# Row norms by powers on GpSimd in place of logarithms and exponentials on ScalarE

## The chip, the cores and the metric

The kernel runs on one core of a Trainium2 chip. The metric is the device time of that core in microseconds (us), as the median of several executions; a profile is one further execution, taken with the hardware profiler. Engines are named as the profile names them: PE (TensorE, matmuls), PEld (its weight loads), DVE (VectorE), ACT (ScalarE), POOL (GpSimd) and SP (SyncE, which here only issues DMAs). Each engine runs its instructions strictly in the order in which they stand in its queue, and waits on semaphores for the others.

## What is computed

Cosine attention over 8 batches of 12 heads with 448 positions of 64 elements, then a feed-forward layer over all 3584 tokens:

```python
def _attn_ref(q, k, v, tau):                       # 8 x 12 x 448 x 64 each
    q_n = q / (np.linalg.norm(q, axis=-1, keepdims=True) + 1e-06)
    k_n = k / (np.linalg.norm(k, axis=-1, keepdims=True) + 1e-06)
    scores = np.matmul(q_n, k_n.transpose(0, 1, 3, 2)) / tau
    scores = scores - np.max(scores, axis=-1, keepdims=True)
    attn = np.exp(scores)
    attn = attn / (np.sum(attn, axis=-1, keepdims=True) + 1e-09)
    return np.matmul(attn, v).astype(np.float32)

def _moe_ref(x, w_in, w_out):                      # 3584 x 768, 768 x 2048, 2048 x 768
    h = x @ w_in
    relu6 = np.clip(h + 3.0, 0.0, 6.0)
    g = h * relu6 / 6.0
    return (g @ w_out).astype(np.float32)
```

What the change touches is the factor 1 / (norm + 1e-6) of each row of q and k, that is, (sqrt(n) + 1e-6) to the power of -1, where n is the row's sum of squares.

## The kernel before

**Units of work.** Heads go in 48 pairs, numbered i. Rows of q and k come in items j: one item is q, or k, of two pairs, four heads, laid out as 128 partitions by 14 rows (2 groups of heads by 7 positions) of 64 elements, 896 elements per partition in fp32. Items 2d and 2d + 1 (q and k of the same two pairs) share the index d, from 0 to 23.

**Steps of an item.** LQ loads it (`load_qk`, line 197, a DMA on SP). SQ squares it (`square`, line 224 on ACT or line 226 on POOL or DVE). RE sums the squares of each row (`reduce`, line 238, DVE) into a tile n2 with 2 x 14 numbers per partition, one half for each item of d. NO makes the factor r from both halves at once (`norms`, lines 254 to 257), so it follows the RE of both items; for d = 0 it is done for each half by itself, on 14 numbers per partition. That is 25 groups in all. NM multiplies the item with r (`normalise`, line 269, on POOL in nearly all cases, on DVE for items 2 and 18) into a bf16 tile nrm. Then the item is transposed: for the first 14 items by PE (TR, line 314, into a PSUM bank that DVE copies out, line 336), later by a DMA on SP (XD, line 325) into tiles tT. CQ, CK and CS copy q and k into place; CS of a later pair is a copy by POOL (line 374, tile km).

**The rest.** SC is the scores' matmul of a pair (line 417), EX its exponential on ACT (line 435), VA the product with v (line 457) and FI the division by the sum (lines 477 and 478). VC casts v to bf16 (line 288, mostly POOL). The feed-forward's first matmul is L568, its activation L577 (ACT) and L583 (DVE); the second one, by a scheme with sums of blocks, is L741, with sums on ACT (L789, L760), DVE (L798, L766) and POOL (L770, L771, L774, three adds in a row; L798 on DVE takes the result of L771). W loads a part of the weights by a DMA on POOL's own queue (line 911). DP and D are matmuls of zeros (lines 923 and 918) that keep PE running where it would wait.

**Order.** The order is written out by hand. Each step appends its instructions to the queues of the engines that do it, in the order in which the steps are called; an instruction waits for what it reads and for the last readers of what it writes. The first stage follows the text `PLAN`, in which tokens are the steps above, such as `NO.4` or `NM.6.p` (item 6 on POOL). The parts around two of the norms:

```python
"SC.3.0.0 EX.2.3 VA.1.2 NO.3 RE.8 SC.3.1.1 CQ.4.v EX.3.0 DP.2 DP.4 EX.3.1 VA.1.3 TR.5.Z SC.3.2.0 W SQ.9.p.0.7",
"EX.3.2 FI.1 CK.4.v BK.0.Y VA.2.0 SC.3.3.1 RE.9 LV.4 EX.3.3 NO.4 VA.2.1 VA.2.2 VA.2.3 SC.4.0.0 EX.4.0 NM.6.p",
```

From pair 18 on (`FIRST`), a loop makes one turn per pair i. In a turn with odd i, NO of d = (i + 3) / 2 is called after SC and EX of pair i, after CS of the next pair and after SQ of item i + 5, and ahead of NM of item i + 3, VC and the POOL part of the feed-forward's sums (`post["p"]`).

Of the kernel before, what the change touches and what calls it, by code (L numbers as in the profile page):

```python
# [8 lines left out]
FP32 = mybir.dt.float32  # L9
BF16 = mybir.dt.bfloat16  # L10
AF = mybir.ActivationFunctionType
ALU = mybir.AluOpType
AX = mybir.AxisListType

EPS = 1e-6
# [46 lines left out]
def kernel(  # L62
# [10 lines left out]
    nc = tc.nc  # L73
# [17 lines left out]
    const = ctx.enter_context(tc.tile_pool(name="const", bufs=1))  # L91
# [47 lines left out]
    def raw_buffer(j):  # L139
# [3 lines left out]
    nrms = [const.tile([128, 7, 2, D], BF16, name=f"nrm{i}", tag=f"nrm{i}") for i in range(3)]  # L143
    n2s = [const.tile([128, 2, 14], FP32, name=f"n2{i}", tag=f"n2{i}") for i in range(2)]
    rs = [
        [const.tile([128, 2, 14], FP32, name=f"{x}{i}", tag=f"{x}{i}") for x in ("ln", "nr", "le", "r")]
        for i in range(2)
    ]
    bias = const.tile([128, 2], FP32, name="bias", tag="bias")
    eps_bias, half_bias = bias[:, 0:1], bias[:, 1:2]  # L150
    ident = const.tile([128, 128], BF16, name="ident", tag="ident")

    PV = psum.tile([128, 2, 512], FP32, name="PV", tag="PV")
# [13 lines left out]
    def needs(*what):  # L167
        for w in what:
            assert w in issued or any(x < 0 for x in w[1:] if isinstance(x, int)), w
# [3 lines left out]
    def whole(op, j, heads):  # L173

        done = halves.setdefault((op, j), set())
        done.update(heads)
        if len(done) == 2:
            issued.add((op, j))
        return len(done) == 2
# [66 lines left out]
    def norms(d, *items):  # L246

        needs(("NM", 2 * d - 4), ("NM", 2 * d - 3))
        items = items or (0, 1)
        for x in items:  # L250
            needs(("RE", 2 * d + x))
        it = slice(items[0], items[-1] + 1)
        ln, nr, le, r = (t[:, it, :] for t in rs[d % 2])
        nc.scalar.activation(out=ln, in_=n2s[d % 2][:, it, :], func=AF.Ln)
        nc.scalar.activation(out=nr, in_=ln, func=AF.Exp, scale=0.5)
        nc.scalar.activation(out=le, in_=nr, func=AF.Ln, bias=eps_bias)
        nc.scalar.activation(out=r, in_=le, func=AF.Exp, scale=-1.0)  # L257
        for x in items:
            issued.add(("NO", d, x))

    def normalise(j, e, *heads):
        d = j // 2
        needs(("NO", d, j % 2), ("TR", j - 3))
        nrm = nrms[j % 3]
        nrm_of[j] = nrm
        heads = heads or (0, 1)
        g = slice(heads[0], heads[-1] + 1)
        n = len(heads)
        engines[e].tensor_tensor(  # L269
            out=nrm[:, :, g, :].rearrange("p c g d -> p g c d"),  # L270
            in0=raw_of[j][:, g, :, :],
            in1=rs[d % 2][3][:, j % 2, :]
            .rearrange("p (g c) -> p g c", g=2)[:, g, :]
            .to_broadcast([128, n, 7, D]),
            op=ALU.mult,
        )
        if whole("NM", j, heads):
            raw_of.pop(j)
# [357 lines left out]
    def firsts(b, *fcs):  # L636
        return [(mm1_unit, b, fc) for fc in fcs]
# [236 lines left out]
    for b in range(2, B - 1):  # L874
        first = firsts(b, *range(FCN))
        for n, x in enumerate([0, 3, 3, 3, 3, 2]):
            i = (b + 1) * HP + n
# [5 lines left out]
            x = 0 if n == 1 else 1 if n in (0, 5) and i > FIRST else 2  # L883
# [6 lines left out]
    f = firsts(b, *range(FCN))  # L890
# [50 lines left out]
    def whole_units(n, engines="av"):  # L941
# [5 lines left out]

    OPS = {
        "LQ": load_qk, "LV": load_v, "W": next_weights, "SQ": square, "RE": reduce, "NO": norms,
        "NM": normalise, "VC": vcast, "TR": transposes, "XD": crossbar, "XB": back_crossbar, "XP": back_two, "CQ": copy_q, "CK": copy_k, "CS": copy_k3, "SC": scores,  # L950
        "EX": exps, "VA": values, "FI": finish_values, "BK": back, "CX": copy_x, "U": unit, "UA": lambda: finish_units("a"), "UV": lambda: finish_units("v"),
        "GL": g_left, "WS": lambda x: weight_sums(str(x), 0, KC), "UU": whole_units, "D": busy, "DP": busy_pv, "OPEN": open_ring,
# [16 lines left out]
        nc.vector.memset(t[0:64, 2:4, 0, :], 0.0)  # L969
    zeros = xT[1][:, 0, :]  # L970
    nc.vector.memset(zeros, 0.0)
    nc.vector.memset(eps_bias, EPS)
    nc.vector.memset(half_bias, 0.5)
    make_identity(nc, ident)
    for t in vx:
# [121 lines left out]
```

## Time and profile before

| | us |
|---|---|
| median of 3 runs | 405.11 (405.05 to 406.0) |
| the profiled execution's own time | 406.65 |
| its span, first to last instruction | 404.9 |

| engine | busy us | share of the span | instructions |
|---|---|---|---|
| PE | 395.2 | 98% | 3696 |
| DVE | 285.1 | 70% | 501 |
| ACT | 278.8 | 69% | 609 |
| POOL | 234.1 | 58% | 228 |

The profile's lines read so: in a group, line of the kernel, engine, operation, written tile and read tiles, shapes (partitions x elements), count, then busy us, mean ns of one, idle us of the engine just before them and who released them. In the timeline, start and duration in us, engine, line, operation and tiles, and in square brackets the idle time before it. In the view by stretch, the time of the stretch and then the busy us of each engine in it, with the number of instructions. In the view of a line, duration in ns as minimum, median and maximum, first and last start in us, and below, who waited for it. The PE clock that was granted is 1.000 on average (1 is full speed).

### The profile page before, as it was taken

To read this page: it belongs to the slowest core of one execution; us is meant where nothing else is said; L and a number is where in the kernel's file an instruction comes from. 1 tells how busy PE (TensorE), PEld (TensorE's weight loads), DVE (VectorE), ACT (ScalarE), POOL (GpSimd) and SP (SyncE) were. 2 spreads that over 40 slices of the span, in tenths; PEclk is the share of its full clock that TensorE was granted. 3 is DMA by queue.
4 is the path that set the end of the run, shared out by engine and by line. 5 is a ranking of instruction groups with operands and counts; after the bars stand their busy time and mean duration, and the time that the engine had idled before them with its cause. 6 is when DMAs were issued, how large, how long until landed. Compare 5 with 4: busy or idle time off the path is not lost.

```text
span 404.9 us, 9617 instructions
## 1 busy us (share of the span) xinstructions
PE 395.2 (98%) x3696; PEld 234.2 (58%) x3696; DVE 285.1 (70%) x501; ACT 278.8 (69%) x609; POOL 234.1 (58%) x228
## 2 busy tenths in 40 slices
PE   7899999999999999999999999999999999999996
PEld 5566565456555555655555556556555556555564
DVE  5888777766978677776857887587656666655663
ACT  5999998888477687687667768768758755225230
POOL 6799645761374986578576874876674600510070
PEclk9999999999999999999999999999999999999999
DMA  8999999979788648777699659966864522130134
GB/s 281 259 245 251 231 226 238 188 118 226 186 212 213 156 109 195 202 201 167 171 203 216 133 145 171 182 185 152 186 158 85 112 45 61 38 87 19 26 74 99
DMA packets 91566, 65.32 MB, mean 161 GB/s; under 512 B 56064, under 2 KB 89984, under 8 KB 91520
## 3 DMA queue, kind: packets, MB, share of 16 engines
q1 hardware_dynamic: 87408, 58.02, 61.5%
q0 software_dynamic: 3712, 6.29, 9.0%
q8 instruction: 29, 0.48, 0.5%
q10 hardware_dynamic: 400, 0.39, 0.3%
q14 instruction: 17, 0.14, 0.1%
HBM read 47.19 MB, written 11.01 MB: 144 GB/s over the span
## 4 chain that ended last, share of the span: by engine, by line
PE 91%; DVE 4%; DMA 2%; issue 1%; SPq 1%; POOL 0%; DVEq 0%; POOLq 0%
PE M L568 24%; PE M L741 17%; PE PV L457 13%; PE Y L568 6%; PE M L417 6%; PE Z L568 5%; PE Y L741 4%; PE Z L741 3%; DMA big<-in_q_dram 2%; PE M L821 2%; PE Z L417 1%; PE Y L417 1%; PE Z L821 1%; PE M L615 1%; DVE w_sum L690 1%
## 5 line engine op out<-in xcount | busy, mean ns | idle before, releaser
L435 ACT ACTIVATE at<-M 128x448 bf16<-128x448 f32 x200 | 99.6, 566 | 16.4 <-PE M L417 14.4
L568 PE MATMUL M<-xT,w_in_sb 128*128 128x448 bf16 x522 | 110.7, 352 | 0.0
L568 PEld LDWEIGHTS <-w_in_sb 128*128 128x128 bf16 x768 | 71.9, 98 | 62.4 <-issue 2.5
L269 POOL TENSOR_TENSOR nrm<-big,r 128x896 bf16<-128x896 f32 (+1 forms) x48 | 80.2, 1675 | 26.7 <-ACT r L257 19.3
L577 ACT ACTIVATE u<-M,bias 128x448 bf16<-128x448 f32 x87 | 56.9, 655 | 24.9 <-PE M L568 24.4
L583 DVE SCALAR_TENSOR_TENSOR gT<-u,M 128x448 bf16<-128x448 bf16 x76 | 46.8, 618 | 38.2 <-ACT u L577 37.7
L226 POOL TENSOR_TENSOR big<-big 128x896 f32<-128x896 f32 (+3 forms) x39 | 63.8, 1636 | 11.2 <-DMA big<-in_k_dram 5.7
L457 PEld LDWEIGHTS <-at 128*128 128x128 bf16 (+1 forms) x1536 | 54.8, 97 | 23.2 <-issue 14.0
L457 PE MATMUL PV<-vx,at 128*128 128x65 bf16 (+1 forms) x1536 | 64.3, 194 | 0.2 <-DVE on L478 0.2
L238 DVE TENSOR_REDUCE n<-big 128x14 f32<-128x896 f32 (+1 forms) x50 | 51.9, 1041 | 5.8 <-ACT big L224 5.0
L374 POOL COPY km<-tT 64x128 bf16<-64x128 bf16 x34 | 12.6, 370 | 57.9 <-DMA tT<-nrm 42.2
L770 POOL TENSOR_TENSOR big<-big 128x384 f32<-128x384 f32 x11 | 12.0, 1087 | 55.0 <-ACT big L789 54.9
L741 PEld LDWEIGHTS <-gT 128*128 128x128 bf16 x288 | 27.8, 98 | 20.7 <-DVE gT L583 1.3
L741 PE MATMUL M<-w_out_sb,gT 128*128 128x384 bf16 x208 | 37.9, 326 | 0.0
L435 ACT ACTIVATE at<-Z 128x448 bf16<-128x448 f32 x49 | 27.6, 563 | 9.9 <-PE M L417 9.8
L478 DVE TENSOR_TENSOR on<-PV,rc 128x512 bf16<-128x512 f32 x48 | 33.2, 691 | 1.7
L288 POOL CAST vx<-big 128x512 bf16<-128x512 f32 x44 | 32.8, 749 | 1.6 <-DMA big<-in_v_dram 1.5
L417 PE MATMUL M<-tT,kz 64*128 64x448 bf16 (+1 forms) x175 | 31.7, 351 | 0.0
L741 PEld LDWEIGHTS <-gs 128*128 128x128 bf16 x224 | 21.6, 98 | 14.5
L568 PE MATMUL Y<-xT,w_in_sb 128*128 128x448 bf16 x132 | 28.6, 353 | 0.0
L435 ACT ACTIVATE at<-Y 128x448 bf16<-128x448 f32 x45 | 25.6, 568 | 3.1 <-PE Z L417 2.9
L741 PE MATMUL M<-w_sum,gs 128*128 128x384 bf16 x144 | 26.3, 326 | 0.0
(133 smaller groups left out, 559.8 us busy)
## 6 DMA issues: line engine op xcount, KB each, us to landing
big<-in_v_dram SPq DMA_DIRECT2D x96, 128.0 KB, 4.4
big<-in_k_dram SPq DMA_DIRECT2D x24, 448.0 KB, 4.9
big<-in_q_dram SPq DMA_DIRECT2D x24, 448.0 KB, 4.0
out_dram<-o SPq DMA_DIRECT2D x107, 96.0 KB, 2.2
w_in_sb<-in_moe_w_in_dram POOLq DMA_DIRECT2D x4, 768.0 KB, 12.0
w_out_sb<-in_moe_w_out_dram POOLq DMA_DIRECT2D x4, 768.0 KB, 9.4
tT<-nrm SPq DMA_TRANSPOSE x34, 3.2
xT<-on SPq DMA_TRANSPOSE x25, 3.7
```

The source lines that it names most:

```text
L226: engines[e].tensor_tensor(out=o, in0=i, in1=i, op=ALU.mult)
L238: nc.vector.tensor_reduce(out=n2s[d % 2][:, j % 2, c], in_=sq[:, :, :, :].rearrange("p g c d -> p (g c) d")[:, c, :], axis=AX.X, op=ALU.add,)
L269: engines[e].tensor_tensor(out=nrm[:, :, g, :].rearrange("p c g d -> p g c d"), in0=raw_of[j][:, g, :, :], in1=rs[d % 2][3][:, j % 2, :] . ...
L288: (engines[e].copy if e == "a" else engines[e].tensor_copy)(out=o, in_=f)
L417: nc.tensor.matmul(o, ks, qt[rows], start=True, stop=True)
L435: nc.scalar.activation(out=o, in_=x, func=AF.Exp, scale=inv_tau)
L457: nc.tensor.matmul(pv_out(j, h), at[rows, n, q_cols(i // HP, j)], vt[rows, 3 + h if name == "M" else 5 * h + int(name[1]), :], start=(name ...
L478: nc.vector.tensor_tensor(out=on[:, :, :, :].rearrange("p j h d -> p h j d"), in0=pv4[:, :, :, 0:D], in1=rc[:, :, :].to_broadcast([128, 2, ...
L568: nc.tensor.matmul(ps[:, 0:S], w_in_sb[:, cc, fc * 128 : (fc + 1) * 128], x[:, cc, 0:S], start=(cc == 0), stop=(cc == CC - 1),)
L577: nc.scalar.activation(out=u[:, :], in_=ps[:, 0:S], func=AF.Relu, bias=half_bias, scale=1.0 / 6.0)
L583: nc.vector.scalar_tensor_tensor(out=g[:, fc, c0 : c0 + S], in0=u[:, :], scalar=1.0, in1=ps[:, 0:S], op0=ALU.min, op1=ALU.mult,)
L741: nc.tensor.matmul(m, lhs[:, c, :], rhs[:, c, c0 : c0 + width], start=(base is None and c == 0), stop=(c == KC - 1), skip_group_check=True,)
```

## The change

`norms` no longer uses ACT. n to the power of 0.5, an addition of 1e-6 and the power of -1 become three instructions on POOL: a tensor_tensor with the exponent broadcast from a column of the tile bias, a tensor_scalar, and a second tensor_tensor. The tile ln goes, and the column that held 1e-6 holds -1.0. The calls of `norms`, and with them its place in the order, stay as they are; the instructions now stand in POOL's queue at that place.

```diff
     rs = [
-        [const.tile([128, 2, 14], FP32, name=f"{x}{i}", tag=f"{x}{i}") for x in ("ln", "nr", "le", "r")]
+        [const.tile([128, 2, 14], FP32, name=f"{x}{i}", tag=f"{x}{i}") for x in ("nr", "le", "r")]
         for i in range(2)
     ]
     bias = const.tile([128, 2], FP32, name="bias", tag="bias")
-    eps_bias, half_bias = bias[:, 0:1], bias[:, 1:2]
+    less_bias, half_bias = bias[:, 0:1], bias[:, 1:2]
...
         it = slice(items[0], items[-1] + 1)
-        ln, nr, le, r = (t[:, it, :] for t in rs[d % 2])
-        nc.scalar.activation(out=ln, in_=n2s[d % 2][:, it, :], func=AF.Ln)
-        nc.scalar.activation(out=nr, in_=ln, func=AF.Exp, scale=0.5)
-        nc.scalar.activation(out=le, in_=nr, func=AF.Ln, bias=eps_bias)
-        nc.scalar.activation(out=r, in_=le, func=AF.Exp, scale=-1.0)
+        nr, le, r = (t[:, it, :] for t in rs[d % 2])
+        half, less = (x.to_broadcast([128, len(items), 14]) for x in (half_bias, less_bias))
+        nc.gpsimd.tensor_tensor(out=nr, in0=n2s[d % 2][:, it, :], in1=half, op=ALU.pow)
+        nc.gpsimd.tensor_scalar(out=le, in0=nr, scalar1=EPS, scalar2=None, op0=ALU.add)
+        nc.gpsimd.tensor_tensor(out=r, in0=le, in1=less, op=ALU.pow)
...
-            in1=rs[d % 2][3][:, j % 2, :]
+            in1=rs[d % 2][2][:, j % 2, :]
...
-    nc.vector.memset(eps_bias, EPS)
+    nc.vector.memset(less_bias, -1.0)
     nc.vector.memset(half_bias, 0.5)
```

## The prediction

> **What bounds the kernel now.** I read the page's busy line and the chain that ended last first, to see which engine sets the end.
>
> ```profile
> PE 395.2 (98%) x3696; PEld 234.2 (58%) x3696; DVE 285.1 (70%) x501; ACT 278.8 (69%) x609; POOL 234.1 (58%) x228
> PE 91%; DVE 4%; DMA 2%; issue 1%; SPq 1%; POOL 0%; DVEq 0%; POOLq 0%
> ```
>
> PE is busy for 395.2 of 404.9 us, and neither ACT nor POOL is on the chain with a share that counts. ACT being relieved can therefore bring nothing beyond PE's idle time, 9.7 us, of which 4 (79.9 less 75.9) lie after 325 us, when the norms are over, and most of the rest before the first matrix work. What can be lost has no such ceiling: PE runs its queue in order, and whatever reaches it late is lost. So the question is who has slack. The busy time by stretch, the two first ones:
>
> ```profile
> core 0: us, PE busy (x) PEld busy (x) DVE busy (x) ACT busy (x) POOL busy (x), PEclk, DMA share, GB/s
> 0.00:12.20 12.20, 8.16 (x51) 5.51 (x52) 7.37 (x30) 7.00 (x15) 8.17 (x23) 1.00 0.86 273
> 12.20:47.00 34.80, 34.07 (x454) 22.13 (x455) 28.18 (x64) 32.88 (x66) 32.73 (x26) 1.00 1.05 251
> ```
>
> From 12.2 to 47 us POOL is busy for 32.73 of 34.80 us, as full as ACT (32.88). The 58% of the page is a mean over a full start, a loop at 144.7 of 208 us and an empty end. The change puts its new work on POOL where POOL has nothing free.
>
> **What goes and what comes.** The four ACT lines, by their view:
>
> ```profile
> L254 ACT ACTIVATE ln<-n x25: 198/236/297, 5.9 to 308.5; 128x28 f32<-128x28 f32 x23, 128x14 f32<-128x14 f32 x2
> L255 ACT ACTIVATE nr<-ln x25: 214/226/227, 6.2 to 308.8; 128x28 f32<-128x28 f32 x23, 128x14 f32<-128x14 f32 x2
> L256 ACT ACTIVATE le<-nr,bias x25: 306/318/319, 6.4 to 309.0; 128x28 f32<-128x28 f32 x23, 128x14 f32<-128x14 f32 x2
> L257 ACT ACTIVATE r<-le x25: 214/226/227, 6.7 to 309.4; 128x28 f32<-128x28 f32 x23, 128x14 f32<-128x14 f32 x2
>   POOL nrm L269: 19.3, 7
> ```
>
> ACT loses 25 x (0.236 + 0.226 + 0.318 + 0.226) = 25 x 1.01 = 25 us. In the full stretch that is five groups, 5 us, but PE's own idle there is 0.73 us, so I count no gain. The 19.3 us that POOL waits for ACT's r fall in idle time of POOL and are worth nothing by themselves.
>
> POOL gains 25 groups of pow, add, pow. No row shows a pow on POOL. The nearest are its multiplies:
>
> ```profile
> L269 POOL TENSOR_TENSOR nrm<-big,r 128x896 bf16<-128x896 f32 x44 | 76.6, 1742 | 24.5 <-ACT r L257 17.0 <-issue 6.4 <-DMA big<-in_v_dram 0.7
> L269 POOL TENSOR_TENSOR nrm<-big,r 128x448 bf16<-128x448 f32 x4 | 3.7, 936 | 2.2 <-ACT r L257 2.2
> ```
>
> The undisturbed 896 takes 1.69 in the timeline, the 448 0.94: (1.69 - 0.94) / 448 = 1.68 ns per element and 0.18 us fixed. So one pass over 28 elements is 0.18 + 0.047 = 0.23 us, the lower bound for a pow, as if it cost what a multiply does. [...] I take 20 steps of 0.047: P = 1.12 us (0.65 for the first two groups, of 14 elements). The count of 20 is my guess, and the largest unknown here; 50 steps, P = 2.5, is the upper end. I give the step the price of a multiply's pass, the nearest row. The add is 0.15 (between the 0.10 of a memset of one element and 0.23). Each dependent step on POOL starts 0.08 after the one before (L770 ends at 282.67 and L771 starts at 282.75). A group holds POOL's queue for G = 2 x 1.12 + 0.15 + 2 x 0.08 = 2.55 us (1.61 for the first two), and its reader starts 0.08 later. All 25: 62 us, POOL at 296 of 405.
>
> [...]
>
> **Where it lands on PE.** POOL runs in order, in the order of the plan's text, so NO now stands in POOL's queue ahead of work that didn't wait for it. The rows, by the timeline, of POOL, DVE, ACT and PE:
>
> ```profile
> 13.26 1.68 POOL L226 TENSOR_TENSOR big<-big 128x896 f32<-128x896 f32 x1 [1.13 <-DVE tT L336]
> 24.00 0.85 POOL L911 DMA_DIRECT2D w_in_sb<-in_moe_w_in_dram  x1
> 24.87 1.69 POOL L226 TENSOR_TENSOR big<-big 128x896 f32<-128x896 f32 x1
> 26.51 1.69 POOL L269 TENSOR_TENSOR nrm<-big,r 128x896 bf16<-128x896 f32 x1
> 27.91 1.07 DVE L238 TENSOR_REDUCE n<-big 128x14 f32<-128x896 f32 x1
> 29.01 0.23 ACT L254 ACTIVATE ln<-n 128x28 f32<-128x28 f32 x1
> 12.19 0.56 PE L314 MATMUL Z<-ident,nrm 128*128 128x128 bf16 x7 [1.57 <-POOL nrm L269]
> 30.13 0.56 PE L314 MATMUL Y<-ident,nrm 128*128 128x128 bf16 x7
> ```
>
> - NO.0 in two halves: POOL is free at 6.26, so NM.1 starts at 7.9 in place of 7.03, the second group starts at 9.66, and NM.0 at 11.35 in place of 10.30. TR.0 (12.19) waits for just that: PE is 1.05 late.
> - SQ.4 at 13.26 follows a load, so it keeps its time. NO.1 starts at 14.9 and NM.3 at 17.5 in place of 14.90; TR.3 (16.64) was waiting for it: 2.6 late in all.
> - NO.2: NM.4 at 21.8 (was 17.32), NM.5 over at 25.2, before TR.5 (26.56) needs it. Hidden by that lead of 6 us.
> - NO.3 stands ahead of a weight load (24.00) and of SQ.9 (24.87). SQ.8 ends at 28.4, NO.3 at 31, so SQ.9 is 6.9 late and its sum RE.9 (27.91) starts at 33.5, ends at 34.6. NO.4 needs RE.9, and NM.6 (26.51), which needs neither, stands behind NO.4: NM.6 starts at 37.1, ends at 38.8. TR.6 (30.13) goes to 38.9: 8.8 late in all. On ACT, ln of NO.4 waited for the same sum (28.98 to 29.01) and nothing of POOL's stood behind it.
> - That wait would bite with pows of no cost too: NM.6 could not start before RE.9 has ended, about 29.3, nor TR.6 before 31.1, 1 us after its time.
> - NM.7 (32.13) is over at 44.5: TR.7 (34.76) 9.8 late. NO.5 stands ahead of NM.8 (34.89, now 48.0): TR.8 (38.38) 11.5 late. The four weight loads on POOL's queue shift with it by 7 to 13 us and are needed by the first matmul of L568 at 43.9, which is itself 11.5 late.
> - NO.6 stands ahead of the cast at 44.56 and of NM.11: TR.11 (53.73) 12.4, and the first L457 behind that cast (68.3) 14.1 late.
>
> From there to 117 us POOL is busy for 35 of 70 us, and a group of 2.55 fits. In the loop, to 325 us, POOL is busy for 144.7 of 208, per two turns (14.7 us) 10.2, so 4.5 are free. Most places have cover, the wait for the transposed keys above all (42.2 us in 8 waits). In an odd turn, NO now stands ahead of the three adds of L770 to L774; where they follow in the same turn, L798 on DVE waits for L771 and PE for the bank that L798 frees. L771 ends at 137.70 and 255.03, L798 starts at 138.06 and 255.45 and runs 0.56, and PE takes the bank at 138.94 and 256.17: 0.3 us of slack against 2.55, so 2.2 us twice. The sum is 14.1 + 2 x 2.2 = 18.5.
>
> The profiled execution took 406.65 us, 1.75 more than its span; the median of the three runs is 405.11. I add the sum to the median: **423.6 us**.
>
> With one step per pow (G = 0.77) the same walk gives 3.2 at TR.8 and 0.45 twice, +4.1. From there to 18.5 a microsecond of G costs eight: five groups up to TR.8, NO.6, and the two turns. Above 2.55 more turns lose their cover, about twelve; above 4.5 the loop's free time is gone and all of its groups count. At 50 steps (G = 5.4) I get +57. A long stall may also cost clock: the 1.57 us at 10.6 left it at 1.00, but the first 18 matmuls of L923 ran at 0.21 us each and 13 later ones at 0.11, so that a fall would cost some 2 us. I count 0, the one shown stall, and keep 2 for the range.
>
> **Rivals.** (1) Faster. PE waits 1.57 us for NM.0, and NO.0's second half sat on ACT behind a square that waited for its load (n was ready at 7.66, ln started at 9.19). On POOL it can start at 8.9. If G for 14 elements is under 0.75, NM.0 starts before 10.30 and PE gains up to 1.2 us there, and up to 0.73 more if ACT paces the start; at most 2, 403.1 us. Against it: TR.3 is set by the load before SQ.4 whatever NM.0 does, and NO.4 stands ahead of NM.6 at any price. Chance 0.05, and 0.03 that gain and loss cancel within 0.3%, about what a measurement of this kernel can tell from no change. (2) The pow is no more than a few passes: only the new waits in the queue are left, +4 to +6, 409 to 411 us; 0.12. (3) POOL becomes the bound: past 50 steps each further microsecond of P costs about 40 of the 50 pows, so that P = 5 gives some +170, 575 us. No row excludes it, as none shows how POOL works out a power; 0.14. (4) The diff could leave the waits on ACT as they are; but its reader is line 269, whose r now comes from POOL, so I give it nothing. The forecast, 6 to 50 steps, keeps 0.66.
>
> **How the numbers follow.** The range runs from 408.5 (one step, less half a microsecond) to 462 (50 steps); left out are the cases that are no slower, 0.08, and POOL as the bound, 0.14. Faster 0.05, same 0.03, slower 0.92.
>
> **What would show it.** Right: two rows of pow on POOL with means near 1.1 us, POOL at some 295 us of busy time, ACT at 254; PE waiting for nrm of POOL several times before 55 us, the longest at TR.6 (about 5 us); DVE waiting for POOL at L798. PE's busy time stays near 395. Wrong: pows under 0.3 us, a start whose TR.6 isn't late, or pows so long that PE waits in each turn of the loop.

## The result and the profile after

The changed kernel takes 583.37 us (median of 5 runs, 582.69 to 584.17) against 405.11 for the kernel before beside it: 1.437 times as long, 95% interval 1.433 to 1.441. The forecast was 423.6, its range ended at 462. The profiled execution of the changed kernel has a span of 581.8, so 176.9 us more than before's 404.9.

The busy line and the chain that ended last, from the page of the changed kernel:

```profile
PE 436.7 (75%) x3696; PEld 250.8 (43%) x3696; DVE 277.0 (48%) x501; ACT 260.4 (45%) x509; POOL 473.5 (81%) x303
POOL 65%; PE 20%; issue 7%; DVE 4%; DMA 2%; ACT 1%; POOLq 0%; SPq 0%; DVEq 0%; ACTq 0%
```

The chain has changed hands: 91% PE before, 65% POOL now. POOL is busy for 473.5 us, 239 more; PE's own busy time has grown by 41.5 with the same 3696 matmuls, as it ran part of them at a lower clock (0.871 in the mean). The two new rows of powers, by the view of their lines (duration in ns as minimum, median and maximum):

```profile
L255 POOL TENSOR_TENSOR nr<-n,bias x25: 2582/4796/4896, 6.3 to 482.2; 128x28 f32<-128x28 f32 x23, 128x14 f32<-128x14 f32 x2
L257 POOL TENSOR_TENSOR r<-le,bias x25: 2612/4815/5177, 9.4 to 487.7; 128x28 f32<-128x28 f32 x23, 128x14 f32<-128x14 f32 x2
```

One power over 28 elements takes 4.81 us, over 14 elements 2.61. A group is 4.80 + 0.29 + 4.82 plus two gaps of 0.08, about 10.1 us, where the forecast had 2.55. The stretches shown of before, now:

```profile
0.00:12.20 12.20, 7.44 (x41) 4.89 (x41) 7.33 (x29) 5.33 (x7) 10.08 (x23) 1.00 0.89 280
12.20:47.00 34.80, 15.78 (x120) 9.23 (x120) 9.31 (x16) 8.94 (x11) 34.05 (x16) 0.66 0.23 65
```

From 12.2 to 47 us POOL is busy for 34.05 of 34.80 us, but with 16 instructions in place of 26, and PE gets 120 matmuls done in place of 454, at a clock of 0.66. The timeline of POOL and PE around NO.4 and TR.6, the place that the prediction had called the longest wait:

```profile
66.29 4.81 POOL L255 TENSOR_TENSOR nr<-n,bias 128x28 f32<-128x28 f32 x1 [1.20 <-DVE n L238]
71.20 0.29 POOL L256 TENSOR_SCALAR le<-nr 128x28 f32<-128x28 f32 x1
71.57 4.82 POOL L257 TENSOR_TENSOR r<-le,bias 128x28 f32<-128x28 f32 x1
76.36 1.68 POOL L269 TENSOR_TENSOR nrm<-big,r 128x896 bf16<-128x896 f32 x1
78.09 0.93 PE L314 MATMUL Y<-ident,nrm 128*128 128x128 bf16 x7 [18.27 <-POOL nrm L269]
```

It reads from the bottom: PE sat idle for 18.27 us until NM.6 (76.36) had ended; NM.6 needs nothing from NO.4, it stands behind it; and NO.4 itself stood idle 1.20 us for the sum of SQ.9, which NO.3 had pushed back. The transposes then take 0.93 us in place of 0.56, at the lower clock.

The same in the loop, by the timeline of POOL, DVE and PE:

```profile
222.58 4.78 POOL L255 TENSOR_TENSOR nr<-n,bias 128x28 f32<-128x28 f32 x1
227.94 4.82 POOL L257 TENSOR_TENSOR r<-le,bias 128x28 f32<-128x28 f32 x1
...
238.13 0.99 POOL L771 TENSOR_TENSOR big<-big,o 128x384 f32<-128x384 f32 x1
239.16 0.56 DVE L798 TENSOR_TENSOR big<-Y,big 128x384 f32<-128x384 f32 x1 [9.10 <-POOL big L771]
239.77 2.72 PE L741 MATMUL Y<-w_sum,gs 128*128 128x384 bf16 x8 [8.74 <-DVE big L798]
```

That is the step L771, L798, bank, PE of the prediction: DVE waits 9.10 us for POOL's add, PE 8.74 for DVE.

It is not the only way from POOL to PE in the loop. DVE takes its instructions in order too: a row sum (L238) waits for a square that POOL makes late, and behind it stands L719, a sum of blocks that the feed-forward's matmuls read. By the timeline of DVE and PE:

```profile
306.30 1.09 DVE L238 TENSOR_REDUCE n<-big 128x14 f32<-128x896 f32 x1 [6.08 <-POOL big L226]
308.14 0.87 DVE L719 TENSOR_TENSOR gs<-gT 128x1024 bf16<-128x1024 bf16 x1
309.07 2.74 PE L741 MATMUL M<-w_sum,gs 128*128 128x384 bf16 x8 [4.78 <-DVE gs L719]
```

PE waits 33 us in five waits for L798 and 28.5 us in eight waits for L719, and shortly ahead of each of the eight DVE had sat idle 4.2 to 6.5 us for a square of POOL's.

The walk of the prediction (each group's delay followed through POOL's queue to PE), gone through again with the measured prices (4.81 and 2.61 for a power, 0.29 for the addition), gives some +159. That is an estimate, and its steps are not listed here. So some 18 of the 176.9 us are not in it; they are the second question of the experiments, beside the price.

### The profile page after: what moved, and what is told of

Same layout as the page of the kernel before. It is cut to its first block, busy times and chain, and to the rows that moved or that the text cites. A ratio compares the mean times of both kernels' runs of the same rounds, so it can differ in the third digit from the quotient of the medians.

```text
span 581.8 us, 9606 instructions
## 1 busy us (share of the span) xinstructions
PE 436.7 (75%) x3696; PEld 250.8 (43%) x3696; DVE 277.0 (48%) x501; ACT 260.4 (45%) x509; POOL 473.5 (81%) x303
## 4 chain that ended last, share of the span: by engine, by line
POOL 65%; PE 20%; issue 7%; DVE 4%; DMA 2%; ACT 1%; POOLq 0%; SPq 0%; DVEq 0%; ACTq 0%
POOL nr L255 19%; POOL r L257 17%; POOL big L226 9%; POOL nrm L269 9%; PE M L568 5%; PE M L741 5%; POOL vx L288 3%; PE PV L457 2%; POOL km L374 2%; POOL le L256 1%; PE Z L741 1%; PE Y L741 1%; DVE n L238 1%; DVE w_sum L690 1%; POOL big L770 1%
## 5 line engine op out<-in xcount | busy, mean ns | idle before, releaser
L255 POOL TENSOR_TENSOR nr<-n,bias 128x28 f32<-128x28 f32 (+1 forms) x25 | 115.6, 4625 | 16.3 <-DVE n L238 16.3
L257 POOL TENSOR_TENSOR r<-le,bias 128x28 f32<-128x28 f32 (+1 forms) x25 | 116.7, 4669 | 2.1
L568 PE MATMUL M<-xT,w_in_sb 128*128 128x448 bf16 x522 | 113.4, 359 | 0.0
L238 DVE TENSOR_REDUCE n<-big 128x14 f32<-128x896 f32 (+1 forms) x50 | 51.9, 1044 | 70.2 <-POOL big L226 67.1
L457 PEld LDWEIGHTS <-at 128*128 128x128 bf16 (+1 forms) x1536 | 62.5, 104 | 41.6 <-issue 33.2
L457 PE MATMUL PV<-vx,at 128*128 128x65 bf16 (+1 forms) x1536 | 72.4, 205 | 9.1 <-POOL vx L288 9.1
L741 PE MATMUL M<-w_sum,gs 128*128 128x384 bf16 x144 | 33.8, 391 | 33.8 <-DVE big L798 24.2
L741 PEld LDWEIGHTS <-gs 128*128 128x128 bf16 x224 | 23.7, 108 | 62.9 <-issue 41.2
L435 ACT ACTIVATE at<-SC 128x896 bf16<-128x896 f32 (+1 forms) x24 | 19.2, 823 | 55.2 <-PE SC L417 53.5
L417 PE MATMUL M<-tT,kz 64*128 64x448 bf16 (+1 forms) x175 | 35.2, 385 | 0.6 <-DVE kz L364 0.6
L314 PEld LDWEIGHTS <-nrm 128*128 128x128 bf16 x98 | 8.4, 127 | 61.2 <-POOL nrm L269 59.6
```

What stands on the lines that cost most here:

```text
L238: nc.vector.tensor_reduce(out=n2s[d % 2][:, j % 2, c], in_=sq[:, :, :, :].rearrange("p g c d -> p (g c) d")[:, c, :], axis=AX.X, op=ALU.add,)
L255: nc.gpsimd.tensor_tensor(out=nr, in0=n2s[d % 2][:, it, :], in1=half, op=ALU.pow)
L257: nc.gpsimd.tensor_tensor(out=r, in0=le, in1=less, op=ALU.pow)
L417: nc.tensor.matmul(o, ks, qt[rows], start=True, stop=True)
L435: nc.scalar.activation(out=o, in_=x, func=AF.Exp, scale=inv_tau)
L457: nc.tensor.matmul(pv_out(j, h), at[rows, n, q_cols(i // HP, j)], vt[rows, 3 + h if name == "M" else 5 * h + int(name[1]), :], start=(name ...
```

## The experiments

The theory: a power costs POOL 157 ns per element of a partition (4.81 less 2.61 us, over 14 elements), the group holds POOL's in-order queue for 10 us, and all that stands behind it comes late, PE last. Its rivals: the way from n to r, 10 us in place of 1, is what hurts, and not the queue; the handing over between engines or the place in the queue hurts, and not the price; and for the 18 us, the clock or a gap in the walk.

**The price taken away.**

```diff
-        nc.gpsimd.tensor_tensor(out=nr, in0=n2s[d % 2][:, it, :], in1=half, op=ALU.pow)
+        nc.gpsimd.tensor_tensor(out=nr, in0=n2s[d % 2][:, it, :], in1=half, op=ALU.mult)
...
-        nc.gpsimd.tensor_tensor(out=r, in0=le, in1=less, op=ALU.pow)
+        nc.gpsimd.tensor_tensor(out=r, in0=le, in1=less, op=ALU.mult)
```

> Both powers of the changed kernel become multiplies (the factor r is then not the norm's inverse; the powers are left out), everything else stays: same engine, same place in POOL's queue, same waits. Theory (the price of a power on POOL, 4.81 us for 28 elements, makes the loss, and the place in the queue alone costs little): the two instructions fall to about 0.23 us, POOL's busy time to 234 + 25 x 0.6 = some 249 us, and what is left is the walk for groups of 0.77 us, +4.1 over the kernel before: 409 us (407 to 411), with PE late at TR.6 and TR.8 and nowhere by more than 3 us. Rival A (moving the norms costs nothing by itself, and taking ACT's 25 us off pays): 403 to 405.5. Rival B (the handing over between DVE, POOL and PE or the waits in the queue make the loss, not the price of a power): stays above 480.

Measured: 410.35 us beside 405.97, ratio 1.011 (1.007 to 1.015). All but 4.4 of the 178 us are gone with the operation alone; engine, place and waits are the changed kernel's. The first theory holds, both rivals fall. What PE still waits for, by its timeline:

```profile
18.13 0.56 PE L314 MATMUL Y<-ident,nrm 128*128 128x128 bf16 x7 [1.96 <-POOL nrm L269]
34.73 0.56 PE L314 MATMUL Y<-ident,nrm 128*128 128x128 bf16 x7 [1.50 <-POOL nrm L269]
40.37 0.93 PE L314 MATMUL Z<-ident,nrm 128*128 128x128 bf16 x7 [1.13 <-POOL nrm L269]
146.06 1.46 PE L741 MATMUL Y<-w_sum,gs 128*128 128x384 bf16 x8 [1.29 <-DVE big L798]
```

These are TR.3, TR.6, TR.7 and the bank in the loop. The profiled execution took 414.53, 4.2 more than the median, so an execution at the median may wait less; POOL's busy time in it is 256.3, where some 249 were expected. In the kernel before, TR.6 had no wait of its own (the row at 30.13 has no bracket), and it waits 1.50 now: the new wait of NO.4 for SQ.9's sum does bite with an operation that costs nothing much, as the prediction said. TR.3's wait has grown from 0.24 to 1.96. TR.7's 0.93 us shows a lowered clock after a wait of 1.13; this comes back below.

**The queue, or the way to r.** ACT makes r as before; POOL does its power, addition and power at the same place, into a tile that nobody reads.

```diff
+        nc.scalar.activation(out=nr, in_=n2s[d % 2][:, it, :], func=AF.Ln)
+        nc.scalar.activation(out=nr, in_=nr, func=AF.Exp, scale=0.5)
+        nc.scalar.activation(out=le, in_=nr, func=AF.Ln, bias=eps_bias)
+        nc.scalar.activation(out=r, in_=le, func=AF.Exp, scale=-1.0)
+        u = dead[:, it, :]
...
-        nc.gpsimd.tensor_tensor(out=nr, in0=n2s[d % 2][:, it, :], in1=half, op=ALU.pow)
+        nc.gpsimd.tensor_tensor(out=u, in0=n2s[d % 2][:, it, :], in1=half, op=ALU.pow)
...
```

> The norms are made on ACT as in the kernel before (25 us of ACT); in addition POOL does the power, the addition and the power at the same place in its queue, into a tile that nobody reads. Theory (the group holds POOL's queue for 10 us and everything behind it, NM of the same and other items, squares and sums, comes late): as slow as the changed kernel, 560 to 585 us, POOL busy some 470 us. Rival (it is the way from n to r that became longer, 10.1 us in place of 1.0, and the readers of r wait for that): no reader waits for these powers, so the time stays near 405 to 420.

Measured: 579.49 us, ratio 1.428 (1.421 to 1.435). Powers that nobody waits for cost 173.5 of the 178 us. It is the occupation of POOL's queue, with the time in which a group stands there waiting for its row sums: the dead powers read n2 as the others do. (The 3.9 us to the changed kernel I haven't traced.)

**The price by itself.** At the end of before's queue, POOL does a row of single operations, each twice.

> The kernel before, and at the end of its queue POOL does a row of operations by themselves, each twice, into a tile that nobody reads any more (the kernel's time means nothing here). Theory (the power is worked out element by element, 0.41 us and 157 ns per element of a partition, from the two sizes seen): 1 element 0.57, 7 elements 1.5, 14 elements 2.6, 28 elements 4.8, 56 elements 9.2, 112 elements 18 us; the exponent -1 the same 4.8; 16 partitions of 28 elements the same 4.8; base and exponent both read as full tiles (2 to the power of 2) the same 4.8; a multiply of 28 elements 0.23, an addition of a constant 0.29. Rival A (a large fixed price, such as a routine that has to be fetched at each call): the second of each pair, and 56 and 112 elements, not much over 5 us. Rival B (the price goes by all elements, over the partitions): 16 partitions at about 1 us. Rival C (the broadcast exponent, read with a step of zero, is the slow part): full tiles well under 4.8.

Measured, by the timeline of POOL at the end of that kernel (start, us):

```profile
399.98 0.58 POOL L1072 TENSOR_TENSOR kz<-kz,bias 128x1 f32<-128x1 f32 x1 [6.94 <-DVE kz L1066]
404.87 4.79 POOL L1075 TENSOR_TENSOR kz<-kz,bias 128x28 f32<-128x28 f32 x1
419.08 18.21 POOL L1077 TENSOR_TENSOR kz<-kz,bias 128x112 f32<-128x112 f32 x1
437.36 4.79 POOL L1078 TENSOR_TENSOR kz<-kz,bias 128x28 f32<-128x28 f32 x1
442.23 4.77 POOL L1079 TENSOR_TENSOR kz<-kz,bias 16x28 f32<-16x28 f32 x1
447.08 4.79 POOL L1080 TENSOR_TENSOR kz<-kz 128x28 f32<-128x28 f32 x1
451.94 0.23 POOL L1081 TENSOR_TENSOR kz<-kz,bias 128x28 f32<-128x28 f32 x1
```

The rows are 1, 28 and 112 elements, then at 28 elements the exponent -1, 16 partitions, both operands as full tiles, and a multiply. From 1 to 112 elements it is (18.21 - 0.58) / 111 = 0.159 us per element and 0.42 fixed; the exponent, the number of partitions and the broadcast make no difference, and the second of each pair takes the same to 0.01 us. The base is 2 in all of them; with the real sums, the changed kernel's two rows of powers have means of 4.80 and 4.85 at 28 elements. All three rivals fall. Per element a power is 0.159 / 0.00168 = 95 times a multiply's pass by the prediction's row.

**Half the price.** One power per group, r = n to the power of -0.5.

```diff
-        nc.gpsimd.tensor_tensor(out=nr, in0=n2s[d % 2][:, it, :], in1=half, op=ALU.pow)
-        nc.gpsimd.tensor_scalar(out=le, in0=nr, scalar1=EPS, scalar2=None, op0=ALU.add)
-        nc.gpsimd.tensor_tensor(out=r, in0=le, in1=less, op=ALU.pow)
+        nc.gpsimd.tensor_tensor(out=r, in0=n2s[d % 2][:, it, :], in1=half, op=ALU.pow)
...
-    nc.vector.memset(half_bias, 0.5)
+    nc.vector.memset(half_bias, -0.5)
```

> One power per group in place of power, addition, power: r = n to the power of -0.5, at the same place (the addition of 1e-6 is left out). A group holds POOL for 4.8 us in place of 10.1. Theory (the loss goes by the time that a group holds POOL's queue): the walk with groups of 4.8 us gives +50, and the stretches of lower clock after PE's waits some 5 to 9 more: 453 to 464 us, POOL busy about 353 us. Rival (a loss in proportion to the time added on POOL: 178 x 120 / 240): 494.

Measured: 461.38 us, +55.4. Half of POOL's new time costs under a third of the loss. The loss isn't linear, as the prediction's slopes of 8, 12 and more per microsecond of G had it.

**Where it is lost.** Powers for the first stage alone, and for the loop alone; ACT's four lines for the rest. The edit of the first kernel, cut short; in the second the condition is d < 11.

```diff
+        if d > 10:
+            nc.scalar.activation(out=nr, in_=n2s[d % 2][:, it, :], func=AF.Ln)
...
```

> Powers on POOL for d = 0 to 10 only (the twelve groups of the first stage); from d = 11 on the four ACT lines of the kernel before. Theory (each group's 10 us count where POOL's queue has no room for them): the walk with the measured prices gives +57 by TR.6 and TR.8, +84 by 135 us of the old time and nothing after; with some 8 us of lower clock, 489 to 498 us. Rival (the start is an exception and the loss goes evenly over the groups: 12 of 25 of 178): 490 to 491, but then POOL's loop groups alone must give 498; the two tell apart only together.

> The four ACT lines for d = 0 to 10, the powers on POOL for d = 11 to 23 only (13 groups in the loop). Theory: nothing is lost before 125 us, then +10 at the first L457 behind a cast and 4 to 11 per two turns, +75 by the walk; with some 8 to 10 us of lower clock, 488 to 492 us. Together with the run of the first stage alone the two losses add up to the changed kernel's 178 within some 5 us. Rival (the loop's idle time on POOL, 4.5 us per two turns, hides part of a group of 10.1, so that only 13 x 5.6 = 73 us are left, without clock): 478. Rival (the loop has cover enough, as the prediction's walk had it for 2.55 us): under 440.

Measured: 499.32 and 489.21 us beside 405.61, +93.7 and +83.6, together 177.3 of 177.8 (583.37 less 405.61). The two parts are separate and add up. The first lies 1.3 us above its range of 489 to 498. Spread evenly over the 25 groups the loss would be 85 and 92; it is 7.8 us per group in the first stage and 6.4 in the loop, so the rival of an even loss falls. The walk has some 84 and 75; both measure 8 to 10 more. The rival by POOL's free time alone (13 x (10.1 - 4.5) = 73) is too low by 11, the walk's 75 by 8 or 9: both leave the clock out, and this run can't tell them apart.

**The 18 us.** Matmuls of zeros fill PE's waits in the first stage of the changed kernel.

```diff
-    "NO.0.0 LV.0 DP.2 SQ.2.a.0.7 NM.0.p.0 RE.3 RE.2 NM.0.p.1 TR.1.Y DP.2 TR.0.Z ...
+    "NO.0.0 LV.0 DP.2 SQ.2.a.0.7 NM.0.p.0 RE.3 RE.2 NM.0.p.1 DP.30 TR.1.Y DP.2 DP.50 TR.0.Z ...
...
-    "DP.2 SC.4.1.1 SQ.10.p.0.7 W SQ.11.p.0.7 EX.4.1 CX.0.v TR.6.Y ...
+    "DP.2 SC.4.1.1 SQ.10.p.0.7 W SQ.11.p.0.7 EX.4.1 CX.0.v DP.150 TR.6.Y ...
```

> The changed kernel with more matmuls of zeros (DP) on PE just ahead of the transposes that wait for nrm: 30 before TR.1, 50 before TR.0, 65 before TR.3, 30 before TR.4, 150 before TR.6, 80 before TR.8, 70 before TR.11, each some 0.105 us at full clock, to fill those waits nearly to their end. Nothing else changes. Theory (after a wait of PE of some 4 us or more the granted clock falls, and the matmuls behind it run at half speed, which cost the 18 us that the walk doesn't hold, 8 of them before 125 us): the clock stays near 1 in the first stage and 4 to 9 us come back: 574 to 579 us. Rival (the 18 us are a gap of the walk, not the clock): 582 to 585, with the clock up and no gain.

Measured: 579.55 us (577.59 to 580.01), ratio to before 1.428 (1.426 to 1.431) where the changed kernel has 1.437: 3.8 us come back by the medians, just below the 4 that were expected. The mean clock rises from 0.871 to 0.923; it doesn't stay near 1 in all of the first stage, as was expected (from 30 to 60 us it is 0.83). TR.6 in this kernel:

```profile
78.04 0.56 PE L314 MATMUL Y<-ident,nrm 128*128 128x128 bf16 x7 [1.96 <-POOL nrm L269]
```

It starts at 78.04, against 78.09 with the clock down, and TR.8 at 96.55 against 96.61: up to there POOL sets the time, and a slow PE only shortens its own wait. The gain appears behind TR.8 (the last matmul of TR.13 starts at 133.6 against 137.4), where PE has work of its own again. So the clock is a real part of the 18 us, but only 3.8 of it are shown; the waits of the loop weren't filled, and 14 us stay unassigned between the clock and what the walk simplifies.

**The clock by itself.** At the end of before, runs of 80 matmuls of zeros with waits of set length between them, made by powers on POOL that rewrite the matmuls' input.

> The kernel before, and at its end (its time means nothing here) eight runs of 80 matmuls of zeros on PE with seven waits between them, each as long as powers on POOL take that rewrite the matmuls' input: 1 element (0.58 us), 7 (1.5), 7 and 1 (2.2), 14 (2.6), 14 and 1 (3.2), 28 (4.8), 56 (9.3), plus some 0.2 us of handing over. Theory (the length of a wait decides whether the granted clock falls, and a fall lasts some 10 us whatever the wait): the clock stays at 1 after the first two, as after the 1.57 us in the kernel before, and falls to 0.5 after those from about 3 us on; a run of 80 takes 17 us at full clock and some 5 us more after a fall. Rival (the clock follows the mean load over a longer time, so that single waits of 5 us between runs of 17 us change nothing): no fall after any but the last.

Measured, by PE's timeline (a run of 80 in each row; the bracket is the wait ahead of it), and by stretches around the wait of 2.79 us (PE busy, instructions, granted clock, DMA share, GB/s):

```profile
456.88 17.43 PE L1070 MATMUL Y<-kz,kz 128*128 128x512 bf16 x78 [2.31 <-POOL kz L1075]
477.11 18.95 PE L1070 MATMUL Y<-kz,kz 128*128 128x512 bf16 x79 [2.79 <-POOL kz L1075]
523.59 19.60 PE L1070 MATMUL Y<-kz,kz 128*128 128x512 bf16 x78 [5.00 <-POOL kz L1075]
552.65 18.73 PE L1070 MATMUL Y<-kz,kz 128*128 128x512 bf16 x79 [9.46 <-POOL kz L1075]
```

```profile
473.41:476.82 3.41, 0.90 (x5) 1.00 0.00 0
476.82:480.23 3.41, 3.12 (x8) 0.50 0.00 0
480.23:483.64 3.41, 3.41 (x18) 1.00 0.00 0
```

Waits of 0.71, 1.70 and 2.31 us leave the run at 17.4 us; from 2.79 on each costs 1.3 to 2.2 us more, and not in order of length: the 9.46 has the smallest price, 1.30, as most of its slow time falls into the wait itself. The rival (a mean over a longer time) falls. The fall lasts 3.41 us after the waits of 2.79 and 3.42 and 6.83 after the two longer ones, not the 10 that was expected; in the changed kernel falls last 3.4 to 17 us, always in multiples of 3.41. And length alone does not decide, as the theory had it. In the kernel with multiplies, by stretches:

```profile
36.87:40.28 3.41, 2.22 (x28) 1.00 1.10 304
40.28:43.69 3.41, 3.32 (x33) 0.50 1.03 183
```

A wait of 1.13 us was enough there, in a stretch in which PE was busy for 2.22 of 3.41 us, while stretches of 1.64 and 2.14 in the kernel with the runs of zeros caused no fall. The wait of 1.96 us at TR.3 in the kernel with multiplies was followed by a fall as well, the 1.57 in the kernel before by none. What a stretch must hold I can't say from these runs.

**The place in the queue.** The kernel with multiplies, with four groups moved in the written order:

```diff
-    "SC.3.0.0 EX.2.3 VA.1.2 NO.3 RE.8 SC.3.1.1 ... SC.3.2.0 W SQ.9.p.0.7",
-    "EX.3.2 FI.1 CK.4.v BK.0.Y VA.2.0 SC.3.3.1 RE.9 LV.4 EX.3.3 NO.4 VA.2.1 ... NM.6.p",
+    "SC.3.0.0 EX.2.3 VA.1.2 RE.8 SC.3.1.1 ... SC.3.2.0 W SQ.9.p.0.7 NO.3",
+    "EX.3.2 FI.1 CK.4.v BK.0.Y VA.2.0 SC.3.3.1 RE.9 LV.4 EX.3.3 VA.2.1 ... NM.6.p",
...
```

> Multiplies in place of the powers, as in the first run, and in the written order four groups move behind work on POOL that doesn't need them: NO.3 behind SQ.9, NO.4 behind NM.7, NO.5 to just ahead of NM.10, NO.6 behind NM.11. Theory (what is left of the first run's 4 to 5 us is the place in POOL's queue: PE's waits of 1.50 us at TR.6 and 1.13 at TR.8, and 1.96 at TR.3, beside the old 1.5 at TR.0): the waits at TR.6 and TR.8 go or shrink below 0.5, the one at TR.3 stays, and the two in the loop (1.29 and 0.34) stay: 407 to 409 us. Rival (three more instructions on POOL cost something wherever they stand): 409.5 to 411.

Measured: 411.52 us, ratio 1.013 (1.009 to 1.016). PE's wait at TR.6 is gone and the one at TR.7 (the 1.13, which the expectation puts down to TR.8) is 0.75, but 0.56 and several of 0.2 to 0.3 are new, and the time didn't fall: it lies above the theory's 407 to 409 and just above the rival's 409.5 to 411. The waits moved as expected, the time not: for the 4 us this order is no cure, and which part of them is the place remains open.

**ACT relieved without POOL.** The logarithm and one exponential on ACT, without and with 1e-12 in the logarithm:

```diff
-        nc.scalar.activation(out=nr, in_=ln, func=AF.Exp, scale=0.5)
-        nc.scalar.activation(out=le, in_=nr, func=AF.Ln, bias=eps_bias)
-        nc.scalar.activation(out=r, in_=le, func=AF.Exp, scale=-1.0)
+        nc.scalar.activation(out=r, in_=ln, func=AF.Exp, scale=-0.5)
```

> The kernel before with two ACT instructions per group in place of four (logarithm, then the exponential with scale -0.5; the addition of 1e-6 is left out): ACT loses half of what the change took off it, 25 x 0.54 = 13.6 us, and the way from n to r gets 0.54 us shorter; POOL's queue stays as it was. Theory (PE sets the end and ACT isn't late anywhere that counts, but PE's wait of 1.57 us for NM.0 is): 404 to 406, no difference that can be measured. Rival (taking work off ACT pays, since it is full from 12 to 47 us): 401 to 403.

> As the two ACT instructions, with 1e-12 added inside the logarithm as its bias, so that a row of zeros gives 1e6 as in the reference: r = (n + 1e-12) to the power of -0.5. The bias makes the logarithm some 0.09 us longer (the two rows of before: 318 against 236 ns). Theory (PE's wait for NM.0 goes, 1.57 us in the kernel before, as NO.0's way is shorter by 0.45 us in each half and POOL takes both halves one after the other): 404 to 405.2, about 1 us under the kernel before. Rival (the gain of the run without the bias was chance): 405.2 to 406.

Measured: 404.61 us, ratio 0.997 (0.995 to 0.999), and 405.16, ratio 0.997 (0.995 to 0.999). About 1 us each under the kernel before beside them (405.61 and 406.02), at the edge of what can be told apart, and the fastest versions here. The second number lies on the border between its theory (to 405.2) and its rival (from 405.2). The second kernel also treats a row of zeros as the reference does. The mechanism is not shown: PE's wait for NM.0 is gone in the profile of the first, but there the load ahead of NO.0's second half came early (its square starts on ACT at 6.94); in the second the square starts at 8.93 and the wait is 2.27, in an execution of 408.09 us, the slowest of 12.

## Why the prediction was wrong

**The step that failed is one term: P.** "I take 20 steps of 0.047: P = 1.12 us" measured 4.81, and "50 steps, P = 2.5, is the upper end" was passed by nearly twice. The number of steps was marked as a guess, but the upper end was a guess too: the nearest row, a multiply's pass, lies below a power (0.23 us against 4.79 measured at 28 elements) and says nothing of the top. Counted in such passes, the element's part of a power is 95, twice the end. No run shows that POOL works a power out in steps, or what a step would cost; what the runs show is the price, 0.42 us and 0.159 us per element.

The range should have reached rival (3), POOL as the bound. Its course came true, but its sum doesn't come out of its own terms: from +57 at P = 2.5, 40 us per microsecond of P make +157 at P = 5, not +170, and +149 at the measured 4.81, where 178 were measured. The text itself says that no row excludes that case; with no bound from above, it deserved a chance near the forecast's, not 0.14.

**The rest of the sum.** The fixed part was 0.18 and is 0.42. The addition was 0.15 and is 0.29. The gaps of 0.08 between dependent steps were right.

**The mechanism held, though not whole.** POOL's order, the new wait of NO.4 ahead of NM.6, the longest wait at TR.6 (18.27 us, where about 5 was forecast) and L771 to L798 to the bank are all in the traces. So, nearly, is the sign given for being wrong, "pows so long that PE waits in each turn of the loop": PE waits 13 times for L798 or L719, as many times as the loop has groups, one in two turns. What the prediction doesn't have is DVE's queue: row sums that wait there for POOL's squares and hold up L719 make 28.5 us of PE's waits, nearly as much as L798. "With one step per pow" the walk gave +4.1 and the kernel with multiplies shows +4.4; as the waits could be moved there without the time falling, this agreement may be luck. The steeper slope past G = 4.5 held as well: +55 at 4.8, +178 at 10.1.

**ACT's 25 us were worth next to nothing**, as counted: taking two of the four ACT lines away without touching POOL moved the time by 0.3%. Nor did ACT's busy time fall by 25: it went from 278.8 to 260.4, where 254 was forecast. Rows of ACT overlap in the timeline (in the kernel before, a square of 0.95 us starts at 8.33 and the logarithm behind it at 9.19): the busy times of ACT's groups, form by form, add up to some 315 us there and 290 in the changed kernel, where the engine's busy time is 278.8 and 260.4.

**The clock was counted at 0**, with 2 us kept for the range, from one wait of 1.57 us. Waits of 2.79 to 9.46 us cost 1.3 to 2.2 us each where PE had work right behind them, and filling seven of them gave 3.8 us back.

## What to carry to other kernels

For an operation that no row of the trace showed, its neighbours gave a lower bound here (0.23 us, against 4.79 measured) and no upper one; measure such an operation alone at two sizes before summing, or give the case in which it becomes the bound its full weight. On an in-order engine ask how long the newcomer holds the queue and what stands behind it, there and in the queues of the engines that wait for it: here powers that nobody read cost nearly as much as powers that were needed, and part of the loss reached PE through DVE's queue. Room in the mean (58% busy) is no room in a stage that is full.

## What the runs showed of the hardware

A power on POOL took 0.42 us plus 0.159 us per element of a partition, from 1 to 112 elements, the same for 16 as for 128 partitions (4.77 and 4.79 us at 28 elements) and for the exponents 0.5, -1 and 2. In the changed kernel PE's granted clock was 1.00 or, in a fall, 0.50, and a fall lasted one to five times 3.41 us. With the runs of zeros, falls came after single waits of 2.79 us and more between dense matmuls and none after 2.31; with the multiplies, they came after waits of 1.13 and 1.96 in looser stretches (PE busy for 2.22 and 1.67 of 3.41 us). At TR.6, where POOL set the time, a fall cost nothing: it came at 78.04 and 78.09 with the clock up and down.
